# An RWKV-6 attention followed by a Hyena gate: the later two thirds of a hand-laid instruction order are laid anew, and the y of chunks 18 to 20 is transposed by DMA

## The chip, the core and the metric

The kernel runs on one core of a Trainium2 chip. The time is the device time of one execution in microseconds (us). Before the change it is 157.04 us, the median of three runs (156.68 to 157.12).

A core has TensorE (PE, matmuls and transposes; its weight loads are listed apart as PEld), VectorE (DVE), ScalarE (ACT), GpSimd (POOL), and SyncE (SP), which here only issues DMAs. Each engine works through its own instructions in program order; an instruction that depends on another engine's result waits for a semaphore, and everything behind it on its engine waits with it.

## What is computed

The inputs are r, k, v, w of shape (4, 8, 768, 48): 4 sequences (b), 8 heads, 768 time steps, head size 48. The first half is a recurrence with a decaying state:

```python
for t in range(S):
    cur = np.einsum('bhd,bhe->bhde', u[None] * kt, vt)
    y[:, :, t] = np.einsum('bhd,bhde->bhe', rt, state + cur)
    state = wt[:, :, :, None] * state + np.einsum('bhd,bhe->bhde', kt, vt)
```

Its output, laid out as x of shape (4, 768, 384), goes into the second half:

```python
proj = x @ w_proj
x1, x2, x3 = (proj[..., :D].copy(), proj[..., D:2 * D].copy(), proj[..., 2 * D:].copy())
X2 = np.fft.rfft(x2, n=S, axis=1)
H = np.fft.rfft(filter_fft, n=S, axis=0)[None, :, :]
x2_conv = np.fft.irfft(X2 * H, n=S, axis=1)
y = x1 * x2_conv * x3
return (y @ w_out).astype(np.float32)
```

## The kernel before, in words

**Tiling.** A sequence is cut into 6 chunks of 128 time steps, so there are 24 chunks, numbered 0 to 23; chunks 18 to 23 are the last sequence, b = 3. A chunk holds all 8 heads, 128 x 384 numbers.

**Chunk work.** For chunk c, four loads (`ldw`, `ldk`, `ldr`, `ldv`, 192 KB each, issued by SP) bring the inputs. ACT takes the logarithm of w (`lw`), PE sums it over time with triangular matrices (`cs`, `ce`), ACT exponentiates (`en`, `eq`, `ph`). `kh` and `q` multiply k and r by these factors, `rk` is r times k, `rku` multiplies by u, `cc` sums it per head, `v` casts v, `vc` is v times that sum. The pair q, kh is transposed: either eight PE transposes into PSUM (`tqk`) and a copy out (`tT` on ACT or DVE), or, for chunks 18 to 23 already before the change, one DMA transpose (`tT` issued by SP). Then `sc` (scores, PE, into a double-size PSUM tile that only `sc` and the last `pA` use), `mt` (masking, DVE, 1024 wide), `kv` and `S` (state on PE and DVE), `y` (PE), `xn` (DVE: y plus vc). `xn` is transposed by three PE transposes (`yt`) and copied into `xT` (ACT or DVE). In the second half of a sequence (chunks 3 to 5 of it) DVE also forms sum and difference with the first half, `sa` and `sb`, straight from the transpose's PSUM tile and from `xT` of the chunk three earlier.

**Sequence work.** For each sequence: `x2` (6 projections of the sums and differences) and `ab` (copies), a forward transform `f` (6 matmul groups), the products with the filter's spectrum `ur`, `ui` and their difference `pp`, the inverse transform `iE`, `iO`, `iP`, the copy `ec`, sum and difference `s`, `d`; beside it the projections `p1` and `p3` with `x1`, `x3` (copies) and `g` (their product); `yy` (or its halves `yl`, `yh`) multiplies by g; `po` (or `pA` with `pB`) is the output projection, `o` the copy out of PSUM and `st` the store. The suffix `.b.fb.hf` of p1 and p3 names sequence, column block and half of the time axis: `p3.3.2.0` is sequence 3, block 2, first half, and reads `xT` of chunks 18, 19 and 20.

**The order.** Nothing is a loop in the emitted program: the string `ORDER` (lines 42 to 141) lists 1103 words, and `emit` (lines 864 to 879) issues them one after the other. `V:mt23` is the operation `mt` on chunk 23 on DVE; P, V, A, G and S stand for PE, DVE, ACT, POOL and SP. `@3` names one of six PSUM banks (`@8` the double-size tile), `+2` adds warm-up matmuls. An operation that may run on several engines is moved by changing its letter. The order of words of one letter is the order on that engine. A PE operation into a bank waits until the readers of that bank's last tile are done; buffers in SBUF rotate (three of most chunk tiles, six load buffers of each input).

Names and lines that are touched: `op_xT` (692 to 699) has a branch for SP, one `dma_start_transpose` of the 128 x 384 tile `xn` into `xT`; `sums` (677 to 684) reads the transpose's PSUM tile for chunks 21 to 23 and `xT` for chunks 18 to 20; `op_tT` (592 to 599) is the DMA transpose of 128 x 1024 that exists before.

```python
        if e == "S":
            nc.sync.dma_start_transpose(
                out=xT_b[b % 2][:, :, ci * L:(ci + 1) * L], in_=xn_b[c % 3]
            )
            return
        copy(e, xT_b[b % 2][:, :, ci * L:(ci + 1) * L], bank_of[f"yt{c}"])
```

Of the kernel before, what the change touches and what calls it, by code (L numbers as in the profile page):

```python
# [53 lines left out]
G:vc2 A:xn1 V:S2 A:lw8 P:sc3@8+2 G:rk5 A:tT4 P:cs6@5 P:kv3@4 V:mt3 P:yt1@1 P:cs8@3 A:en6 G:kh5
P:y2@2 A:m2c5 V:xT1 P:ce6@5 V:cc4 G:vc3 P:sc4@8 A:v4 V:S3 A:xn2 G:vc4 V:mt4 A:en8 P:yt2@0+5
A:eq6 P:y3@1 G:rku5 A:xT2 S:ldv5 P:m2t1@4 V:q6 P:cs7@2 A:xn3 P:m2t4@3 G:kh6 P:ce8@0 A:en7 S:ldk7
P:ce7@1 V:m2c4 A:eq8 V:cc5 P:y4@2 A:eq7 V:rk6 P:m2t3@3 S:ldr7 A:ph7 A:m2c1 P:tqk5@1 A:xn4
P:tqk6@4 S:ldw9 A:tT5 P:yt3@2 V:fs S:ldv6 A:ph6 A:tT6 P:kv4@1 P:yt4@5 V:fd P:sc5@8 S:ldwp1
A:m2c3 G:kh7 V:sa4 P:hf4@4+5 V:sa3 V:S4 P:hf3@3 G:v5 V:sb3 A:ph8 V:sb4 A:lw9 P:hf1@1 S:ldr8
# [24 lines left out]
A:ab.1.0.1 V:cc12 P:yt11@0 S:ldr15 P:kv12@1 A:x1.1.2.0 P:x2.1.0.0@3 V:sa11 A:xT10 V:S12
P:iE.0.1@2 A:ab.1.0.0 S:ldv14 P:iO.0.1@4 V:sb11 G:q14 V:mt12 P:ce15@5 A:xT11 P:x2.1.0.2@1 A:lw17
S:ldv15 G:rku13 P:p1.1.2.1@3 A:eq15 V:rk14 P:ce17@0 P:sc13@8 A:x1.1.2.1 S:ldw18 P:iP.0.1 A:ph15
A:eq17 V:yy.0.0 G:rku14 P:x2.1.1.1@3 A:ab.1.0.2 V:cc13 S:ldr16 P:p1.1.0.1@5 A:v13 V:mt13
P:x2.1.1.2@0 A:ec.0.1 G:kh14 S:ldwo A:x1.1.0.1 P:kv13@1 A:ab.1.1.1 P:p1.1.1.1@2 V:s.0.1 G:q15
A:lw16 P:p3.1.2.0@5 V:S13 A:ab.1.1.2 P:f.1.0@3 V:d.0.1 A:x1.1.1.1 G:vc13 P:cs16@1 V:g.1.2.0
A:v14 P:cs17@0 P:ce16@4 V:ur.1.0 G:kh15 S:ldk16 A:en17 P:tqk14@2 A:en16 P:p3.1.0.0@5 A:tT14  # L90
V:yy.0.1 G:vc12 S:ldk17 P:y12@0 P:tqk15@1 V:cc14 P:p3.1.2.1@3 A:eq16 V:g.1.0.0 S:ldr17 G:rk15
A:v15 P:y13@2 V:tT15 A:ph16 P:kv14@5 A:lw18 V:xn12 P:sc14@8 S:ldk18 G:q16 P:cs18@4 V:xn13 A:cwo
P:f.1.2@1 V:g.1.2.1 S:ldw19 G:rku15 P:yt13@0 V:S14 P:yt12@2 A:en18 P:f.1.5@3 V:ur.1.1 A:xT13
G:rk16 S:ldv18 P:po.0.5@5 A:vc14 P:kv15@4 V:ui.1.2 P:po.0.4@0 G:kh16 S:ldv16 P:po.0.1@1 V:S15
G:rku16 P:p3.1.1.1@3 S:ldv17 V:mt14 A:o.0.4 P:po.0.3@4 A:o.0.5 G:kh18 P:f.1.4@0 S:ldw20 A:xT12
V:cc15 A:o.0.1 P:sc15@8 V:cc16 G:rk17 A:o.0.3 P:ce18@5 S:ldr18 P:y14@2 A:lw19 V:ur.1.2
P:po.0.0@1 A:eq18 G:rku17 S:ldk19 A:v18 P:tqk16@4 V:g.1.1.1 A:o.0.0 P:f.1.1@0 V:xn14 G:kh17
A:tT16 S:ldk20 P:ce19@3 V:mt15 P:yt14@1 P:f.1.3@2 A:xT14 G:vc15 S:ldr19 A:v16 P:cs19@4 V:ui.1.0
P:p3.2.1.0@1 G:q17 A:en19 P:sc16@8 S:ldw21 A:eq19 V:ui.1.1 P:p3.2.2.0@4 A:ph18 A:v17 G:vc16
P:y15@0 A:x3.2.1.0 S:ldv19 V:cc17 P:p1.2.1.0@5 A:lw20 G:q18 V:xn15 P:po.0.2@2 A:ph19 A:x3.2.2.0  # L100
S:ldr20 V:mt16 A:x1.2.1.0 P:tqk17@1 G:rk18 A:o.0.2 P:yt15@3 P:p1.2.0.0@0 S:tT18 A:tT17 V:sa15
P:ce20@4 V:pp.1.2 P:kv16@5 A:x1.2.0.0 V:pp.1.0 P:p3.2.0.0@2 G:kh19 A:eq20 V:sb15 S:ldw22
P:kv18@1 P:sc17@8 V:S16 A:lw21 P:y16@0 V:S18 A:ph20 G:vc17 A:xT15 S:ldw23 P:x2.2.1.0@5 V:mt17
A:x3.2.0.0 P:ce21@4 G:rku18 A:ab.2.1.0 P:iO.1.0@1 P:cs20@3 A:eq21 P:p1.2.2.0@2 V:xn16 A:en20
G:q19 P:p3.1.0.1@5 V:cc18 A:x1.2.2.0 P:y17@0 V:pp.1.1 A:ph21 A:vc18 G:rk19 S:tT19 P:yt16@3
P:iO.1.2@2 V:xn17 P:iE.1.2@4 V:sa16 P:iE.1.0@0 V:sb16 G:g.2.2.0 P:sc18@8 S:ldk21 V:g.1.0.1
P:iP.1.2 A:xT16 S:st.0.1 V:mt18 P:iP.1.0 G:q20 S:ldv20 A:ec.1.2 P:x2.2.0.0@5 S:ldv22 A:ec.1.0
P:yt17@3 P:x2.2.1.1@4 G:rku19 A:ab.2.0.0 V:s.1.2 A:v19 S:st.0.3 P:iE.1.1@0 V:s.1.0 P:iO.1.1@5
A:ab.2.1.1 G:rk20 V:sa17 S:ldr21 P:sc19@8 A:lw23 V:d.1.0 P:iP.1.1 A:lw22 V:sb17 P:kv19@4 G:kh20
V:d.1.2 S:ldv21 A:ec.1.1 P:x2.2.0.1@1 A:xT17 V:S19 P:cs21@2 G:yy.1.0 P:x2.2.1.2@0 A:ab.2.0.1  # L110
V:cc19 S:ldr22 A:en21 P:ce22@3 V:s.1.1 P:y18@4 A:ab.2.1.2 P:cs22@1 S:tT20 P:p1.2.0.1@2 V:xn18
A:v20 P:x2.2.0.2@0 A:eq22 V:d.1.1 G:vc19 A:x1.2.0.1 P:p3.2.2.1@4 V:mt19 A:ph22 A:ab.2.0.2
G:rku20 P:yt18@5 S:ldk22 P:cs23@2 A:en22 P:p1.2.2.1@3 A:x3.2.2.1 V:yy.1.1 G:rk21 P:kv20@0
# [818 lines left out]
```

## Time and profile before

| | |
|---|---|
| median of three runs | 157.04 us |
| the profiled execution | 157.1 us, of which 155.4 us from the first to the last instruction |
| busy: PE / DVE / ACT / POOL | 144.5 / 138.3 / 128.2 / 115.9 us |
| instructions: PE / DVE / ACT / POOL | 1540 / 264 / 306 / 134 |
| moved by DMA | 28.98 MB in 112038 packets, 106641 of them under 512 B |
| mean granted TensorE clock | 0.973 |

The busy time of an engine is the time in which at least one of its instructions runs. Instructions of one engine overlap a little (a matmul group that lasts 0.65 us is followed by the next 0.49 us after its start), so a busy share near 100% does not say that there is no short wait. SP is not counted as busy; its rows (SPq) show how long the issue of a DMA takes, and the listing of DMA issues shows how long it takes from the issue to the landing. The chain of waits follows the work that ended last back from its end: at each step to what released it, or to the instruction before it on its engine.

### The profile page before, as it was taken

The numbers are of one execution on the slowest core, as the hardware profiler recorded it, in microseconds if no ns is written. First come the engines' busy times: TensorE is split into PE (matmuls) and PEld (weight loads), VectorE is DVE, ScalarE is ACT, GpSimd is POOL, SyncE is SP. The second block draws the span as 40 slices with busy tenths as digits, with TensorE's granted clock in tenths as the row PEclk, the third lists the DMA queues.
The fourth block names the chain that finished last, engine by engine and source line by source line (L and its number), as shares of the span: only waits on it lengthen the run. The fifth ranks groups of instructions, "written<-read, shape, count | busy, mean of one in ns | idle before, by whom it ended". The sixth has DMA issues, their size and how long they took to land.

```text
span 155.4 us, 4177 instructions
## 1 busy us (share of the span) xinstructions
PE 144.5 (93%) x1540; PEld 90.8 (58%) x1540; DVE 138.3 (89%) x264; ACT 128.2 (82%) x306; POOL 115.9 (75%) x134
## 2 busy tenths in 40 slices
PE   6969988968999999999999999999999999999990
PEld 3446565756465666656757666775666566555440
DVE  6537879979989999999999999999999989999950
ACT  3279659969698899989999999999999877677470
POOL 7200869892999899799969999699999998900600
PEclk9985799999999999999999999999999999999997
DMA  5999979999999999899999999978999986000575
GB/s 96 196 202 183 207 148 197 195 286 226 244 172 281 253 178 200 170 192 211 190 200 259 170 181 210 189 147 141 227 209 228 206 175 222 2 0 0 181 281 203
DMA packets 112038, 28.98 MB, mean 186 GB/s; under 512 B 106641, under 2 KB 112018, under 8 KB 112018
## 3 DMA queue, kind: packets, MB, share of 16 engines
q1 hardware_dynamic: 112018, 28.72, 84.4%
q8 instruction: 12, 0.20, 0.6%
q14 instruction: 8, 0.07, 0.1%
HBM read 22.41 MB, written 4.72 MB: 175 GB/s over the span
## 4 chain that ended last, share of the span: by engine, by line
PE 63%; DMA 12%; DVE 11%; ACT 5%; SPq 5%; issue 2%; DVEq 0%
PE p L705 13%; DMA ldw<-in_w_dram 9%; PE x L735 6%; PE po L850 6%; PE f L421 5%; SPq L452 5%; PE sc L607 3%; PE f L413 3%; PE tqk L588 3%; DMA ldv<-in_v_dram 3%; PE iE L792 3%; PE iO L781 3%; PE iE L781 2%; PE yt L675 2%; DVE mt L614 2%
## 5 line engine op out<-in xcount | busy, mean ns | idle before, releaser
L505 POOL TENSOR_TENSOR qk<-ldr,eq 128x384 bf16<-128x384 f32 x20 | 21.3, 1067 | 11.4 <-ACT F L357 10.3
L705 PE MATMUL p<-xT,wproj 128*128 128x384 bf16 x144 | 29.3, 326 | 0.1
L614 DVE TENSOR_TENSOR mt<-sc,mask_excl 128x1024 bf16<-128x1024 f32 x24 | 29.2, 1216 | 0.0
L502 POOL TENSOR_TENSOR qk<-ldk,en 128x384 bf16<-128x384 f32 x21 | 22.4, 1067 | 4.1 <-PE kv L625 2.7
L508 POOL TENSOR_TENSOR rk<-ldr,ldk 128x384 bf16<-128x384 f32 x19 | 19.8, 1042 | 1.8 <-issue 1.5
L560 POOL TENSOR_TENSOR rku<-rk,u_bc 128x384 bf16<-128x384 bf16 x19 | 18.0, 945 | 2.5 <-DVE rk L508 1.3
L462 ACT ACTIVATE lg<-ldw 128x384 bf16<-128x384 f32 x24 | 12.6, 530 | 8.6 <-DMA ldw<-in_w_dram 7.5
L705 PEld LDWEIGHTS <-wproj 128*128 128x128 bf16 x144 | 13.0, 97 | 8.2 <-issue 1.0
L582 POOL TENSOR_TENSOR vc<-v,cc 128x384 bf16<-128x384 bf16 x19 | 16.5, 867 | 0.7 <-DVE cc L566 0.5
L757 DVE TENSOR_TENSOR filt<-f,HF 128x768 bf16<-128x768 f32 x18 | 16.6, 952 | 0.1
L735 PE MATMUL x<-wproj,sd 128*128 128x384 bf16 x72 | 14.9, 326 | 0.3 <-DVE HF L435 0.2
L276 ACT ACTIVATE qkT<-tqk 128x1024 bf16<-128x1024 bf16 x13 | 13.3, 1027 | 0.1
L276 ACT ACTIVATE v<-ldv 128x384 bf16<-128x384 f32 x23 | 12.2, 530 | 1.3 <-DMA ldv<-in_v_dram 1.3
L276 ACT ACTIVATE x<-p 128x384 bf16<-128x384 f32 x24 | 11.7, 499 | 1.8 <-PE p L705 1.6
L726 POOL TENSOR_TENSOR g<-g,x 128x384 bf16<-128x384 bf16 x8 | 7.1, 912 | 8.1 <-DVE g L278 8.1
L276 ACT ACTIVATE ab<-x 128x384 bf16<-128x384 f32 x24 | 11.7, 500 | 1.2 <-PE x L735 0.9
L484 ACT ACTIVATE en<-cs 128x384 f32<-128x384 f32 x24 | 11.9, 500 | 0.9 <-PE cs L466 0.7
L490 ACT ACTIVATE eq<-ce 128x384 f32<-128x384 f32 x24 | 11.5, 494 | 0.6 <-PE ce L478 0.6
L588 PE MATMUL tqk<-ident,qk 128*128 128x128 bf16 x144 | 11.5, 230 | 0.2 <-ACT phi L496 0.2
L632 DVE TENSOR_TENSOR S<-kv,phi 128x384 bf16<-128x384 f32 x20 | 10.9, 550 | 0.3 <-PE kv L625 0.2
L566 DVE TENSOR_REDUCE cc<-rku 128x8 f32<-128x384 bf16 x21 | 11.1, 541 | 0.0
L276 ACT ACTIVATE xT<-yt 128x384 bf16<-128x384 bf16 x20 | 9.9, 495 | 1.3 <-PE yt L675 0.6
(158 smaller groups left out, 397.0 us busy)
## 6 DMA issues: line engine op xcount, KB each, us to landing
ldw<-in_w_dram SPq DMA_DIRECT2D x24, 192.0 KB, 4.0
ldk<-in_k_dram SPq DMA_DIRECT2D x24, 192.0 KB, 4.2
ldr<-in_r_dram SPq DMA_DIRECT2D x24, 192.0 KB, 3.9
ldv<-in_v_dram SPq DMA_DIRECT2D x24, 192.0 KB, 4.0
out_dram<-o_all SPq DMA_DIRECT2D x24, 192.0 KB, 2.2
raw<-in_moe_w_proj_dram SPq DMA_DIRECT2D x3, 576.0 KB, 5.8
filt<-in_moe_filter_fft_dram SPq DMA_DIRECT2D x1, 1152.0 KB
P<-in_moe_w_out_dram SPq DMA_DIRECT2D x1, 576.0 KB, 5.0
```

What stands on the lines that cost most here:

```text
L276: nc.scalar.activation(out=o, in_=i, func=AF.Copy)
L462: nc.scalar.activation(out=o, in_=i, func=AF.Ln)
L502: two(e).tensor_mul(qk_b[c % 3][:, 1, :, 0:D], ld["k"][c % 6], en_b[c % 3])
L505: two(e).tensor_mul(qk_b[c % 3][:, 0, :, 0:D], ld["r"][c % 6], eq_b[c % 3])
L508: two(e).tensor_mul(rk_b[c % 2], ld["r"][c % 6], ld["k"][c % 6])
L560: two(e).tensor_mul(rku_b[c % 2], rk_b[c % 2], u_bc)
L582: two(e).tensor_mul(o, v, s.to_broadcast([L, H, D]))
L588: nc.tensor.transpose(p[:, x, j, :], qk_b[c % 3][:, x, 2 * j:2 * j + 2, :], ident)
L614: nc.vector.tensor_mul(mt_b[c % 3], bank_of[f"sc{c}"].rearrange("p q j t -> p (q j) t"), dataclasses.replace(m[:, :], ap=[m[:, :].ap[0], [ ...
L705: nc.tensor.matmul(p, wproj[:, cb, col0:col0 + L], xT_b[b % 2][:, cb, sl], start=(cb == 0), stop=(cb == CB - 1),)
L735: nc.tensor.matmul(p, sd_b[q][0][:, cb, ti * L:(ti + 1) * L], wproj[:, cb, C:2 * C], start=(cb == 0), stop=(cb == CB - 1),)
L757: two(e).tensor_mul(U_all[:, part, n], dataclasses.replace(f, ap=[f.ap[0], [0, 2]] + list(f.ap[1:])), HF[:, n, part:part + 2, :],)
```

## The change

Only the string `ORDER` changes. Its first 280 words, up to `A:ab.0.0.0`, stay in their order; in them 34 PE words, from `cs3` on, get other bank numbers. The 823 words behind them become 820 and are laid in another order on every engine. Three words are gone, `P:yt18`, `P:yt19` and `P:yt20`, nine PE transposes in all, and the words `A:xT18`, `A:xT19`, `A:xT20` become `S:xT18`, `S:xT19`, `S:xT20`. Other words that change engines, from the first letter to the second:

- ACT to POOL: v7, v13, vc14, vc18. ACT to DVE: ab.3.0.0, x1.3.0.1, x3.3.2.1, o.3.2, o.3.3.
- DVE to ACT: xT6, tT15, xT22, X.3.4, x3.3.1.1, ec.3.0, o.3.0.
- DVE to POOL: rku8, pp.0.1, q11, rk14, pp.1.0, g.2.1.0, g.3.0.1, g.3.1.0, g.3.2.1, yl.3.1, yh.3.1.
- POOL to DVE: pp.0.0, q13, rk13, yy.0.2, rku17, rk18, rku18, q20, g.2.0.1, g.3.1.1, yl.3.0.

The banks, the beginning of the new part, and the stretches in which the DMA transposes stand, before and after:

```diff
-G:rk3 V:cc0 V:rT1 P:sc1@8 V:vc0 S:ldw7 P:kv0@0 G:q4 P:rt2@4 P:cs3@3 P:m2t2@1 V:rT2 P:cs4@2 A:en3
+G:rk3 V:cc0 V:rT1 P:sc1@8 V:vc0 S:ldw7 P:kv0@0 G:q4 P:rt2@4 P:cs3@1 P:m2t2@2 V:rT2 P:cs4@3 A:en3
...
-P:x2.0.1.0@3 A:ab.0.0.0 V:cc7 P:sc7@8 A:v7 V:sb5 P:x2.0.0.1@0 S:ldr9 V:xn6 G:rk8 P:x2.0.0.2@2
+P:x2.0.1.0@4 A:ab.0.0.0 S:ldr9 G:rk8 S:ldv8 S:ldw10 P:x2.0.0.2@0 A:ab.0.1.0 P:x2.0.0.1@3 G:q8
...
-P:p3.2.1.1@4 V:xn19 P:po.1.1@5 V:ui.2.2 G:rku21 S:tT21 P:p3.2.0.1@0 P:sc20@8 V:ur.2.2 G:rk22
-A:x3.2.0.1 P:po.1.3@1 S:st.0.0 A:o.1.1 P:yt19@3 V:mt20 S:ldr23 P:po.1.4@0 G:pp.2.2 A:xT19
-S:st.0.5 P:kv21@2 A:o.1.3 S:ldk23 P:f.2.0@5 V:cc21 A:o.1.4 P:y20@3 V:ur.2.0 A:vc21 P:po.1.2@1
-G:kh22 P:po.1.0@0 V:xn20 P:po.1.5@5 G:q22 V:S21 P:yt20@3 P:sc21@8 V:pp.2.0 A:xT20 G:rku22
-P:f.2.2@2 S:tT22 A:o.1.2 V:mt21 A:o.1.0 P:f.2.3@3 A:x3.2.1.1 P:p1.3.1.0@1 G:q23 S:ldv23 V:ur.2.1
-P:p1.3.2.0@0 A:x1.3.1.0 G:kh23 P:y21@4 A:o.1.5 P:iO.2.0@1 A:v22 V:xn21 P:p1.3.0.0@2 G:rk23
-S:tT23 V:ui.2.1 P:iO.2.1@5 A:x1.3.0.0 P:yt21@4 P:sc22@8 A:x1.3.2.0 V:sa21 G:rku23 P:iE.2.1@2
...
+A:ab.2.1.1 V:xn18 P:p1.2.0.1@3 V:s.1.0 S:xT18 P:p1.2.2.1@4 G:rku20 A:x1.2.0.1 V:d.1.0 P:iO.1.1@0
+A:v20 V:d.1.2 P:kv19@3 G:yy.1.0 A:lw23 S:tT20 P:iE.1.1@5 V:cc20 A:x1.2.2.1 P:p3.2.2.1@2 V:cc19
+A:x1.2.1.1 P:sc19@8 V:S19 S:ldk22 P:iP.1.1 V:yy.1.2 P:x2.2.1.2@4 G:rk21 S:ldr22 A:ec.1.1 V:mt19
+P:p3.2.0.1@1 A:x3.2.2.1 S:st.0.0 P:kv20@3 A:x3.2.0.1 S:ldk23 P:x2.2.0.1@5 G:vc19 V:s.1.1
+A:ab.2.1.2 P:ce22@2 S:st.0.5 A:ab.2.0.1 V:S20 P:ce23@1 G:rku21 P:f.2.4@4 S:st.0.4 A:eq22 V:d.1.1
+P:sc20@8 S:st.0.1 A:ph22 V:ur.2.2 G:kh21 A:eq23 P:f.2.1@5 S:ldv21 A:vc20 P:y19@3 V:yy.1.1 G:kh22
+P:f.2.5@0 V:xn19 P:po.1.0@2 V:mt20 S:xT19 P:cs23@1 P:p3.2.1.1@4 G:q22 A:en23 P:po.1.5@3 A:o.1.0
+V:cc21 P:po.1.4@1 A:x3.2.1.1 G:kh23 S:tT21 V:ui.2.2 A:o.1.5 P:y20@2 A:o.1.4 P:po.1.2@4 G:rk22
+V:xn20 P:f.2.0@3 A:v21 V:ui.2.0 S:xT20 P:f.2.3@0 G:rk23 A:vc21 V:ur.2.0 P:f.2.2@1 G:pp.2.2
+P:kv21@2 S:st.0.3 P:po.1.1@5 V:ui.2.1 S:tT22 P:po.1.3@3 A:o.1.1 V:S21 P:sc21@8 V:ur.2.1 G:q23
+P:p3.3.2.0@0 S:ldv22 P:p3.3.1.0@5 S:st.0.2 V:mt21 G:rku23 P:p1.3.2.0@2 S:tT23 A:x3.3.1.0
+P:p1.3.0.0@1 A:x1.3.2.0 G:rku22 P:p1.3.1.0@5 V:cc23 A:x1.3.0.0 S:ldv23 V:pp.2.0 P:y21@2
+G:g.2.0.0 A:x1.3.1.0 P:sc22@8 S:st.1.5 V:xn21 A:o.1.3 P:p3.3.0.0@1 A:x3.3.2.0 S:st.1.0 V:mt22
...
+P:iP.2.1 G:g.3.1.0 P:y22@4 A:ec.2.0 P:x2.3.1.0@5 A:ec.2.1 V:xn22 G:vc23 P:y23@1 A:ab.3.1.0
+V:s.2.1 P:iE.2.2@0 G:g.2.2.0 P:yt22@4 V:xn23 P:iO.2.2@5 P:iP.2.2 V:sa22 G:g.2.1.1 V:d.2.1
```

More of the change, by code (lines that the diff above doesn't have):

```diff
@@ L54 @@
[L54 to L59, printed above, removed]
@@ L84 @@
[L84 to L89, printed above, removed]
@@ L90 @@
[L90 to L113, printed above, removed]
@@ new lines @@
+A:ab.0.0.2 V:xn6 P:ce9@1 A:ab.0.0.1 P:sc7@8 V:sb5 S:ldwp2 V:cc7 P:yt6@4 A:xT5 G:rku8 P:f.0.1@0
+V:mt7 A:eq9 P:x2.0.1.1@2 A:xT6 G:v7 P:tqk8@3 A:cwp0 G:kh9 V:ui.0.0 P:x2.0.1.2@5 S:ldw13
+P:f.0.0@4 A:ab.0.1.2 G:rk9 V:cc8 P:kv7@0 A:ab.0.1.1 V:ur.0.0 P:p1.0.0.1@5 S:ldr10 A:ph9 A:v8
+G:vc7 P:f.0.2@2 A:lw10 V:pp.0.0 S:ldk10 A:x1.0.0.1 P:f.0.3@1 G:rku9 A:tT8 V:ur.0.1 P:f.0.5@4
+S:ldw11 P:p1.0.0.0@5 G:q9 V:ui.0.1 P:y7@3 A:x1.0.0.0 P:p1.0.1.0@2 S:ldw12 A:cwp2 V:xn7 G:vc8
+P:p1.0.2.1@5 V:ui.0.2 P:yt7@1 S:ldk11 P:f.0.4@3 G:pp.0.1 A:x1.0.1.0 P:sc8@8 A:xT7 V:S7 P:ce10@4
@@ new lines @@
+P:y14@1 P:f.1.4@0 V:ur.1.0 S:ldk18 G:vc14 A:cwo P:tqk16@3 V:ur.1.2 P:p3.1.1.1@4 G:rku16 S:ldw22
+P:ce18@2 A:tT16 P:sc15@8 V:xn14 G:rk17 P:po.0.2@0 V:S14 S:ldr18 A:v15 P:yt14@1 V:g.1.1.1
+P:po.0.4@3 A:eq18 G:q17 V:mt15 A:xT14 P:po.0.1@5 S:ldw20 A:o.0.4 P:kv15@4 A:lw19 G:kh17
+P:p1.2.0.0@1 V:cc15 S:ldk19 A:v16 P:sc16@8 V:pp.1.2 A:ph18 A:o.0.2 G:vc15 P:tqk17@3 A:x1.2.0.0
+V:mt16 S:ldk20 P:p3.2.2.0@2 A:o.0.1 P:y15@0 G:kh18 A:x3.2.2.0 P:ce19@1 S:ldv17 V:S15 A:tT17
+P:p1.2.1.0@5 V:rku17 G:pp.1.0 P:cs19@2 P:f.1.3@4 V:xn15 S:ldr19 A:eq19 V:cc16 A:en19 P:f.1.2@3
@@ new lines @@
+V:ui.1.1 A:x1.2.1.0 S:ldv18 P:p3.2.1.0@0 A:ph19 A:lw21 P:kv16@2 G:q18 V:ur.1.1 A:x3.2.1.0
+P:p3.2.0.0@5 S:ldr20 A:lw22 P:yt15@1 P:po.0.3@4 A:lw20 V:S16 G:vc16 S:tT18 P:y16@0 V:sa15
+A:o.0.3 V:rk18 P:cs22@3 G:kh19 P:sc17@8 A:v17 V:sb15 P:ce20@2 V:xn16 A:xT15 P:p3.1.0.1@4 V:rku18
+A:eq20 G:q19 S:ldv20 P:po.0.5@0 A:x3.2.0.0 V:cc17 P:po.0.0@1 A:o.0.5 S:ldv19 V:g.1.0.1
+P:p3.1.2.0@5 A:ph20 A:v18 G:vc17 V:mt17 P:cs21@0 A:o.0.0 P:p1.2.2.0@2 S:ldw23 A:en22 G:rk19
+P:x2.2.1.0@4 A:x1.2.2.0 V:g.1.2.0 P:cs20@1 P:y17@3 S:ldr21 V:q20 A:en20 G:rku19 P:ce21@2 V:xn17
@@ L141 @@
+V:s.3.1 P:iP.3.2 S:st.2.5 V:d.3.0 G:yl.3.1 P:po.2.1@3 V:d.3.1 A:ec.3.2 P:po.2.4@4 V:yl.3.0
+A:o.2.1 G:yh.3.0 V:s.3.2 P:po.2.3@1 A:o.2.4 S:st.2.1 P:pA.3.2@0 V:yl.3.2 A:o.2.3 G:yh.3.1
+P:pA.3.0@5 S:st.2.4 V:d.3.2 P:pB.3.0 P:pB.3.2 S:st.2.3 P:pA.3.1@3 A:o.3.0 V:o.3.2 P:pB.3.1
+P:pA.3.4@8 S:st.3.0 V:yh.3.2 A:o.3.1 P:pB.3.4 S:st.3.2 P:pA.3.3@4 A:o.3.4 S:st.3.1 P:pB.3.3
+A:o.3.5 V:o.3.3 S:st.3.4 S:st.3.3 S:st.3.5
 """
```

99 lines of the change are left out of this document (52 added, 47 removed).

## The prediction

> **What bounds the kernel now.** I read the page's shares first, then the stretches of the later two thirds, then the chain of waits backwards from its end.
>
> The page: busy times, the DMA slices, shares of the chain, and two rows of the DMA issues (last figure: median us from issue to landing).
>
> ```profile
> PE 144.5 (93%) x1540; PEld 90.8 (58%) x1540; DVE 138.3 (89%) x264; ACT 128.2 (82%) x306; POOL 115.9 (75%) x134
> DMA  5999979999999999899999999978999986000575
> PE 63%; DMA 12%; DVE 11%; ACT 5%; SPq 5%; issue 2%; DVEq 0%
> ldv<-in_v_dram SPq DMA_DIRECT2D x24, 192.0 KB, 4.0
> out_dram<-o_all SPq DMA_DIRECT2D x24, 192.0 KB, 2.2
> ```
>
> The stretch from the first re-laid word to the end of the last score masking (mt of chunk 23), and from there to the last copy (us, busy time of each engine, clock, DMA share, GB/s):
>
> ```profile
> 47.10:131.04 83.94, 83.47 (x953) 53.98 (x953) 82.30 (x139) 79.51 (x201) 78.24 (x79) 1.00 0.96 204
> 131.04:151.76 20.72, 20.13 (x151) 10.79 (x147) 18.45 (x44) 13.92 (x31) 7.98 (x10) 1.00 0.25 89
> ```
>
> In 83.9 us PE is busy 83.5, DVE 82.3, ACT 79.5, POOL 78.2, and the DMA engines 96%. Nothing stands idle, so a new order has little idle time to win, and what is moved off one engine lands on another that is almost as full. The granted clock is 1.00 throughout, so it is no term of the sum.
>
> The chain from 115.9 us to the end (start, duration, what):
>
> ```profile
> 115.90 0.49 PE f L421 x3
> ...
> 118.78 0.17 PE yt L675 x3
> ...
> 131.26 0.33 PE iO L781 x2
> ...
> 132.99 0.49 PE x L735 x3
> ...
> 151.00 0.18 PE pA L842
> 151.18 0.02 issue
> 151.20 0.56 DVE o_all L278
> ```
>
> It never leaves PE from 115.90 to 151.18: over the last 35 us PE runs from one group to the next, and no other engine ends a wait that lasts. Here too are the paces of PE (start to start): 0.49 for a projection of three matmuls, 0.33 for an inverse half, 0.17 for the three transposes of one y.
>
> **The change, part by part.** I counted the words of each engine in both orders and gave each the duration of its own row. DVE, POOL and ACT groups, from 47.9 us on (busy us, mean ns of one | idle before):
>
> ```profile
> L771 DVE TENSOR_TENSOR P<-filt 128x768 bf16<-128x768 bf16 x9 | 5.9, 675 | 0.0
> L812 DVE TENSOR_TENSOR raw<-raw,g 128x768 bf16<-128x768 bf16 x7 | 3.9, 566 | 0.2
> L505 DVE TENSOR_TENSOR qk<-ldr,eq 128x384 bf16<-128x384 f32 x1 | 0.9, 887 | 0.0
> L278 DVE COPY xT<-yt 128x384 bf16<-128x384 bf16 x2 | 0.7, 342 | 0.0
> L278 DVE COPY qkT<-tqk 128x1024 bf16<-128x1024 bf16 x1 | 0.7, 681 | 0.0
> L508 DVE TENSOR_TENSOR rk<-ldr,ldk 128x384 bf16<-128x384 f32 x1 | 0.6, 550 | 0.0
> L560 DVE TENSOR_TENSOR rku<-rk,u_bc 128x384 bf16<-128x384 bf16 x1 | 0.5, 533 | 0.0
> L757 DVE TENSOR_TENSOR filt<-f,HF 128x768 bf16<-128x768 f32 x18 | 16.6, 952 | 0.1
> ```
> ```profile
> L560 POOL TENSOR_TENSOR rku<-rk,u_bc 128x384 bf16<-128x384 bf16 x15 | 14.3, 954 | 2.5 <-DVE rk L508 1.3 <-DVE cc L566 1.0
> L582 POOL TENSOR_TENSOR vc<-v,cc 128x384 bf16<-128x384 bf16 x13 | 11.2, 859 | 0.6 <-DVE cc L566 0.5
> L771 POOL TENSOR_TENSOR P<-filt 128x768 bf16<-128x768 bf16 x3 | 4.9, 1640 | 0.6 <-DVE filt L757 0.6
> ```
> ```profile
> L276 ACT ACTIVATE v<-ldv 128x384 bf16<-128x384 f32 x16 | 8.5, 530 | 0.0
> L276 ACT ACTIVATE xT<-yt 128x384 bf16<-128x384 bf16 x17 | 8.4, 496 | 1.3 <-PE yt L675 0.6 <-DVE sd L690 0.4
> L578 ACT ACTIVATE vc<-v,cc 128x48 bf16<-128x48 bf16 x32 | 7.6, 326 | 0.1
> ```
>
> *Bank numbers in the first third.* The order there stays and each bank's former tile is emptied no later than before, so I take 0. A bank that came free late would cost at most one ACT copy, 0.5 us; as PE also waits for other things, 0 to 0.5.
>
> *PE.* Three transposes of y fall away: 3 x 0.17 = 0.5 us less. Nothing is added.
>
> *ACT.* Less: xT 18 to 20 (3 x 0.496), v7 and v13 (2 x 0.530), vc14 and vc18 (32 short instructions for four chunks took 7.6, so 1.9 each), five copies of some 0.5 in the tail. More: tT15 (1.0) and six copies. Net 4.8 us less. ACT does not stand in the late chain, so I count 0 of it; if its copies free PSUM banks earlier, that is the second rival.
>
> *POOL.* rku8, vc14, vc18, pp.1.0 and two v come to it, yy.0.2, rku17, rku18, rk18 and q20 leave; with the tail some 2.5 us more in all, about 1 of it ahead of the last vc. It is idle 83.94 - 78.24 = 5.7 us in the stretch, which covers that; without the cover vc comes late for xn, at 1 us.
>
> *DVE.* Ahead of mt23 five words are added: yy.0.2 0.566, rku17 and rku18 2 x 0.533, rk18 0.550, q20 0.887, together 3.07. Four leave: tT15 0.681, rku8 0.533, one pp 0.675, xT6 0.342, together 2.23. q, rk and pp words that only trade places cancel. Net +0.8 ahead of mt23. In the tail four short products, a store copy and others leave, and five copies and products come: some 0.9 less behind mt23. DVE's total does not change, but its work is moved ahead of the hand-over to PE.
>
> *The hand-over at the end.* DVE and PE around it, by start and duration (the L668 row is xn20, the first L614 row mt21, the second mt23; the PE rows begin y21 and y23):
>
> ```profile
> 121.17 0.55 DVE L668 TENSOR_TENSOR xn<-y,vc 128x384 bf16<-128x384 f32 x1
> ...
> 122.63 1.23 DVE L614 TENSOR_TENSOR mt<-sc,mask_excl 128x1024 bf16<-128x1024 f32 x1
> ...
> 129.83 1.21 DVE L614 TENSOR_TENSOR mt<-sc,mask_excl 128x1024 bf16<-128x1024 f32 x1
> ```
> ```profile
> 122.19 0.40 PE L607 MATMUL sc<-qkT 48*128 48x128 bf16 x8
> ...
> 124.60 0.21 PE L640 MATMUL y<-S,qkT 128*128 128x96 bf16 x1
> ...
> 131.43 0.20 PE L640 MATMUL y<-S,qkT 128*128 128x96 bf16 x1
> ```
>
> mt23 ends at 131.04 now and y23 starts 0.4 later, when PE is free: PE decides. With 0.8 more ahead, and DVE's own waits as they are, mt23 ends at 131.9. PE has less ahead of y23: 0.5 for the transposes, and one projection and one inverse half moved behind y23 against one projection moved ahead, 0.3; it is ready at 131.43 - 0.8 = 130.6 and waits. So y23 starts 0.45 later, with 0.3 more work behind it: the end moves by +0.8.
>
> *The DMA transposes.* The transpose that exists, from the rows of its line (issue, ns min/median/max; then us to landing, min/median/max):
>
> ```profile
> L594 SPq DMA_TRANSPOSE qkT<-qk x6: 1238/1547/1996, 98.5 to 125.4; - x6
> DMA to landing us min/median/max: 3.0/3.8/4.1
> ```
>
> xT is three eighths of its size. No row shows this size; its landing lies between a store's 2.2 and 4.1 us. I take 3.0, nearest to the tT rows, which use the same path. xT18 and xT19 have the same first reader, p3.3.2.0, and are issued 3 us or more earlier, which hides them. xT20 is the tight one: xn20 ends at 121.72 now; with +0.8 and the two L757 products that move behind it (2 x 0.95, less their overlap) it ends at about 120.9. xT20 lands at 123.9 (123.1 to 125.0). p3.3.2.0, the first reader, follows sc21 directly; PE reaches it near 123.0, and its bank (0) is free only after ui.2.1, three L757 products after xn20, at 123.5. So PE stalls 0.4 for the landing (0 to 1.5). Five projections then lead to y21 at 126.3, 1.7 later than now, with three projections fewer behind it (1.5): +0.2, and +1.3 if it lands at 125.0. This runs beside the hand-over and is not added to it; the later of the two sets the end.
>
> [...]
>
> *The SP queue.* Now xn18 on DVE, two issues of loads (the first is ldv21) and the start of kv21:
>
> ```profile
> 111.17 0.56 DVE L668 TENSOR_TENSOR xn<-y,vc 128x384 bf16<-128x384 f32 x1
> ```
> ```profile
> 110.42 0.70 SPq L452 DMA_DIRECT2D ldv<-in_v_dram  x1
> ...
> 114.09 0.58 SPq L452 DMA_DIRECT2D ldk<-in_k_dram  x1
> ```
> ```profile
> 119.27 0.33 PE L623 MATMUL kv<-S,ident 128*128 128x384 bf16 x1
> ```
>
> xT18 waits for xn18. Six DVE words of about 0.47 (cc19, S19, two s, two d) move behind xn18 and 0.9 comes ahead of it, so it ends near 111.73 - 1.9 = 109.8. Behind xT18 stand tT20, ldk22, ldr22, four stores, ldk23 and ldv21. With 0.5 to 0.6 for an issue and 1.5 for tT20, ldv21 issues at about 115.8 and lands 4.0 later at 119.8; v21 (0.53) is ready at 120.3. kv21 has 2 us more PE work ahead of it than now (three f, three po and y20 come ahead, two po and two yt go) and starts near 121.3. The cover is 1 us, so I take 0.
>
> Sum: the profiled execution's 157.1 us + 0.8 (hand-over) = 157.9; its 157.1 lies 0.06 over the median, so 157.8 for the median.
>
> **The rivals.**
>
> *The DMA queue takes the place.* With an issue of 2.0 for each of xT18 and tT20 and a landing of 4.1, ldv21 arrives 1.7 later than above, kv21 stalls 0.7, and xT20 then holds tT22, ldv22 and tT23 behind it: together with xT20's +1.3 the end moves by about +2.0: 159.1. For it: DMA slices at 8 and 9 up to 131 us, and one SP queue. Against it: the last loads have 3 us to spare on the way to y23.
>
> *Faster: PE decides, not DVE.* The deciding point is mt23 before 130.6. From 47.1 on 105 groups at 0.49, 24 halves at 0.33 and the shorter words at their paces in the chain add up to some 98 us, and PE takes 151.18 - 47.1 = 104, so some 6 us are short waits. If ACT's 4.8 us spare empties banks earlier and takes 0.7 us off these, DVE too is fed earlier, and mt23 no longer holds PE. Then -0.5 (transposes) - 0.7: 155.9. For it: the chain is all PE. Against it: DVE's 98% in the stretch.
>
> *No change.* The new waits and the saved transposes cancel (-0.5 against +0.5): 157.1.
>
> **How the numbers follow.** Slower by the hand-over 0.40 (157.3 to 158.5 on its own), by the DMA queue 0.14, no change 0.19, faster 0.27. A change of 0.3% (0.5 us) is about what a measurement of this kernel can tell from none. Some of the hand-over case lies within that, and some of the no-change case outside it: faster 0.29, same 0.20, slower 0.51. The range for 8 in 10 goes from 155.8 (the faster rival) to 159.3 (the queue rival and a little of the bank bound).
>
> **What would show it.** Right: mt23 ends later than 131.3, y23 follows it at once, and the chain steps from PE to DVE between 120 and 134 us. The transpose step is right if p3.3.2.0 starts within 0.5 us of ui.2.1's end and xT lands in about 3 us. Wrong if mt23 ends before 130.6, if PE's late chain has loads or xT in it for over 1 us, or if POOL's vc ends the waits of xn.

## The result and the profile after

The changed kernel takes 158.25 us (median of 20 runs, 156.87 to 161.31) and the kernel before 156.91 us (20 runs, 155.90 to 158.03) on the same chip: a ratio of 1.0084, 95% interval 1.0059 to 1.0110. The change makes the kernel 0.8% slower. On two other chips the same comparison gave 1.0142 (1.0087 to 1.0197) and 1.0125 (1.0073 to 1.0177). Medians are of all executions, while a ratio leaves out those more than 1.5% above the fastest of their kernel on that chip, so it need not be the quotient of the two medians beside it.

The first profile of the changed kernel is of the longest of these executions (161.31 us); the lines below are from a later one, e1b, of 157.65 us. From the page: busy times, the DMA slices, the shares of the chain.

```profile
PE 142.5 (91%) x1531; PEld 89.4 (57%) x1531; DVE 140.8 (90%) x262; ACT 123.3 (79%) x287; POOL 120.1 (77%) x138
DMA  5999999999999999999899898992799794003493
PE 35%; DVE 28%; POOL 12%; issue 8%; DMA 7%; ACT 5%; SPq 2%; POOLq 0%; DVEq 0%; ACTq 0%
```

ACT moved as the counts said (4.9 us less); POOL has 4.2 us more, where 2.5 were counted. PE's 2.0 us less lie in the first third: in the two stretches below it is busy for 103.8 us, before for 103.6. VectorE is 2.5 us busier (1.2 against a second profile of before), which the counts did not say, and the chain has 28% of VectorE where it had 11%. The DMA row ends in 3493 where it ended in 0575: the last slices are fuller.

The same two stretches as before the change, from 0.5 us into x2.0.1.0, the last PE group of the unchanged first third, to the end of mt23, and from there to the last copy (us, busy time of PE, PEld, DVE, ACT, POOL, clock, DMA share, GB/s):

```profile
44.43:130.11 85.68, 83.55 (x946) 53.16 (x945) 85.29 (x141) 75.04 (x182) 80.90 (x83) 1.00 0.95 200
130.11:151.21 21.10, 20.22 (x145) 10.81 (x143) 17.96 (x40) 14.07 (x32) 9.89 (x11) 1.00 0.27 97
```

Up to mt23 VectorE now stands idle for 0.4 us of 85.7; it was 1.6 of 83.9. PE waits for 2.1 us there instead of 0.5. PE's waits of over 0.15 us in this stretch (who waits, for whom: total, times, longest), before and changed:

```profile
PE cs L466 <- DVE g L728: 0.2, 1, 0.2
```
```profile
PE yt L675 <- DVE xn L668: 1.0, 3, 0.5
PE po L850 <- DVE xn L668: 0.5, 1, 0.5
PE po L850 <- DVE raw L812: 0.4, 1, 0.4
PE tqk L588 <- ACT xT L276: 0.2, 1, 0.2
```

So PE waits for VectorE's xn and yy (L812) for 1.9 us, where it waited 0.2. The chain, late part:

```profile
113.77 0.96 DVE filt L757
114.73 1.33 DVE raw L812
116.11 0.50 PE po L850 x2
...
122.42 2.53 PE p L705 x15
124.95 0.98 DVE P L771
125.92 0.48 DVE xn L668
126.45 0.34 PE yt L675 x3
...
147.91 0.35 PE pA L842
148.48 2.05 DMA out_dram<-o_all
150.65 0.56 DVE o_all L278
```

Two things are to be seen. Between 113 and 126 us the chain steps from PE to VectorE and back. And the end is no longer PE's: a copy into o_all (150.65) waits for a store that was issued at 148.48 and had to land first. mt23 (L614) and the start of y23 (the first L640 row):

```profile
128.90 1.21 DVE L614 TENSOR_TENSOR mt<-sc,mask_excl 128x1024 bf16<-128x1024 f32 x1
```
```profile
130.21 0.21 PE L640 MATMUL y<-S,qkT 128*128 128x96 bf16 x1
```

y23 starts 0.1 us after mt23's end at 130.11; it was 0.4 before. The absolute times can't be set beside those of before: the first third, whose words are the same in all kernels here, puts the group x2.0.1.0 anywhere between 43.8 and 48.3 us in the profiles. What can be compared is the length of pieces. In the table, "middle" is the first stretch above, "y23 to PE" goes from the start of y23 to the end of PE's last group, "PE to land" from there to the landing of the last store (issue plus landing of the single stores). "Packet" says whether an instruction packet (8 KB; the trace lists it among the DMA packets as "q14 instruction") was read while the last three stores ran, "last lands" is the landing time of the last store.

| kernel | middle | DVE busy in it | y23 to PE | PE to land | packet | last lands |
|---|---|---|---|---|---|---|
| before (page) | 83.94 | 82.30 | 19.74 | 3.11 | no | 2.07 |
| before, again | 84.92 | 83.79 | 19.74 | 3.37 | no | 2.08 |
| changed, first profile | 84.94 | 84.50 | 20.15 | 4.21 | yes | 2.89 |
| changed, e1 | 85.91 | 84.58 | 20.13 | 4.41 | yes | 2.88 |
| changed, e1b (shown above) | 85.68 | 85.29 | 20.15 | 4.19 | yes | 2.89 |
| e2 own slots | 85.82 | 84.54 | 20.15 | 3.97 | yes | 2.86 |
| e3 three DVE words less | 84.96 | 83.31 | 20.13 | 3.11 | no | 2.01 |
| e4 before, y by DMA | 87.75 | 84.43 | 19.74 | 3.44 | no | 2.07 |
| e5 order only | 84.81 | 84.27 | 19.85 | 4.17 | yes | 3.07 |
| e6 tail of before | 83.29 | 82.73 | 20.41 | 3.08 | no | 2.06 |
| e6b, again | 84.29 | 83.42 | 20.41 | 3.08 | no | 2.07 |
| e8 before, tail of changed | 84.61 | 82.91 | 19.95 | 3.09 | no | 1.98 |
| e9 two stores less | 85.07 | 84.11 | 20.52 | 4.04 | yes | 2.92 |
| e10 words back on POOL | 84.92 | 84.24 | 19.95 | 4.00 | no | 2.06 |

### The profile page after: what moved, and what is told of

It is laid out like the page before. It is cut to its first block, busy times and chain, and to the rows that moved or that the text cites. A ratio compares the mean times of both kernels' runs of the same rounds, so it can differ in the third digit from the quotient of the medians.

```text
span 159.6 us, 4165 instructions
## 1 busy us (share of the span) xinstructions
PE 144.7 (91%) x1531; PEld 90.9 (57%) x1531; DVE 140.3 (88%) x262; ACT 123.9 (78%) x287; POOL 119.7 (75%) x138
## 4 chain that ended last, share of the span: by engine, by line
PE 39%; DVE 26%; DMA 13%; SPq 6%; issue 5%; POOL 4%; ACT 3%; DVEq 0%; ACTq 0%; POOLq 0%
PE p L705 7%; DMA ldv<-in_v_dram 6%; DVE mt L614 6%; SPq L452 6%; PE x L735 6%; DMA ldw<-in_w_dram 5%; DVE filt L757 5%; PE po L850 5%; PE f L421 3%; DVE xn L668 3%; PE f L413 2%; PE iE L792 2%; PE iE L781 2%; PE iO L781 2%; DVE raw L812 2%
## 5 line engine op out<-in xcount | busy, mean ns | idle before, releaser
L614 DVE TENSOR_TENSOR mt<-sc,mask_excl 128x1024 bf16<-128x1024 f32 x24 | 29.1, 1210 | 0.0
L582 POOL TENSOR_TENSOR vc<-v,cc 128x384 bf16<-128x384 bf16 x21 | 18.0, 858 | 3.8 <-DVE cc L566 2.0
L508 POOL TENSOR_TENSOR rk<-ldr,ldk 128x384 bf16<-128x384 f32 x18 | 18.6, 1036 | 1.8 <-DMA ldr<-in_r_dram 1.8
L560 POOL TENSOR_TENSOR rku<-rk,u_bc 128x384 bf16<-128x384 bf16 x18 | 17.4, 970 | 2.2 <-DVE rk L508 1.7
L726 POOL TENSOR_TENSOR g<-g,x 128x384 bf16<-128x384 bf16 x10 | 9.0, 921 | 7.9 <-DVE g L278 7.9
L276 ACT ACTIVATE qkT<-tqk 128x1024 bf16<-128x1024 bf16 x14 | 14.3, 1022 | 0.6 <-PE tqk L588 0.5
L276 ACT ACTIVATE v<-ldv 128x384 bf16<-128x384 f32 x21 | 11.1, 529 | 2.6 <-DMA ldv<-in_v_dram 2.6
L276 ACT ACTIVATE xT<-yt 128x384 bf16<-128x384 bf16 x19 | 9.3, 494 | 3.4 <-DVE sd L690 2.6
L276 ACT ACTIVATE x<-p 128x384 bf16<-128x384 f32 x23 | 11.0, 496 | 1.0 <-PE p L705 0.9
L850 PE MATMUL po<-wout,raw 128*128 128x384 bf16 x54 | 10.9, 326 | 0.9 <-DVE xn L668 0.5
L276 ACT ACTIVATE ab<-x 128x384 bf16<-128x384 f32 x23 | 10.8, 497 | 0.7 <-PE x L735 0.3
```

Source lines behind the costliest of these rows:

```text
L276: nc.scalar.activation(out=o, in_=i, func=AF.Copy)
L508: two(e).tensor_mul(rk_b[c % 2], ld["r"][c % 6], ld["k"][c % 6])
L560: two(e).tensor_mul(rku_b[c % 2], rk_b[c % 2], u_bc)
L582: two(e).tensor_mul(o, v, s.to_broadcast([L, H, D]))
L614: nc.vector.tensor_mul(mt_b[c % 3], bank_of[f"sc{c}"].rearrange("p q j t -> p (q j) t"), dataclasses.replace(m[:, :], ap=[m[:, :].ap[0], [ ...
L850: nc.tensor.matmul(p, y_b[b % 2][:, cb, ti * L:(ti + 1) * L], wout[:, cb, :], start=(cb == 0), stop=(cb == CB - 1),)
```

## The experiments

The theories: the *hand-over* (VectorE has more ahead of mt23), the *tail* (the late stores of sequence 2 hold the end), and the *DMA queue* (transposes of y hold loads or PE).

**e1, the changed kernel again.** No edit.

> The changed kernel itself, for its time and a second profile. Before to after was 156.9 to 158.2 us. Hand-over theory (DVE has more work ahead of mt23, and PE waits for it): mt23 ends 0.8 to 1.0 us later than in before (131.04), y23 starts within 0.2 us of its end, and the last TensorE group ends about 0.8 to 1.1 later than 151.17. Tail theory (the stores of sequence 2 are issued so late that the last copies wait for their landings in the same slots of o_all): from the end of the last TensorE group to the last landing it is 4.2 us against 3.1 in before, so some 1.1 us of the loss lies behind TensorE's last group.

159.64 us, 1.0142 of before. mt23 ends at 131.39 and y23 starts 0.1 after it; PE's last group ends at 151.62. PE to land is 4.41. The tail is there in every profile of the changed kernel; the middle floats by 1 us.

**e2, own slots for the last copies.**

```diff
+    def o_slot(b, ti):
+        if b == 3:
+            return ld["k"][ti].rearrange("p h d -> p (h d)")
+        return o_all[:, ti, :]
...
-        copy(e, o_all[:, ti, :], bank_of[f"po.{b}.{ti}"])
+        copy(e, o_slot(b, ti), bank_of[f"po.{b}.{ti}"])
...
-        nc.sync.dma_start(out=out[b, ti * L:(ti + 1) * L, :], in_=o_all[:, ti, :])
+        nc.sync.dma_start(out=out[b, ti * L:(ti + 1) * L, :], in_=o_slot(b, ti))
```

> The changed kernel, same order, but sequence 3's output tiles go through the slots of the dead k loads, so that no copy o.3.x waits for a store of sequence 2. Tail theory: the waits of the last copies on store landings go (1.4 and 1.6 us in the profile of after) and the time falls by 0.5 to 1.1 us, to about 157.3. Hand-over theory alone: mt23 and the last TensorE group are where they were, the last stores only queue behind the others, and the time moves by less than 0.3 us.

159.37 us, 1.0119 (1.0076 to 1.0162): within 0.3 us of e1. The waits of the copies on landings are gone (the last copy ends 0.6 after PE's last group instead of 1.1), but PE to land falls only from 4.41 to 3.97. The waits alone are not the tail: the last five stores, which no longer wait, land in 2.9 to 3.0 us each.

**e3, less work on VectorE ahead of mt23.** The words V:rku17, V:rk18 and V:rku18 are taken out of the order.

> The changed kernel without three words that the change laid onto VectorE ahead of mt23: rku17, rku18 (0.533 each) and rk18 (0.550). These products are left out, so chunks 17 and 18 take stale values; everything else is as in after. Hand-over theory: 1.6 us less of DVE work ahead of mt23, so mt23 ends at least 0.8 us earlier and the time falls by 0.8 to 1.2 us (157.0 to 157.4), until TensorE decides. Tail theory: the end behind TensorE's last group keeps its 4.2 us, so the time falls no more than the last group does. DMA queue theory: ldv21 and xT20 decide, and the time moves by less than 0.3 us.

159.02 us, 1.0106 (1.0046 to 1.0166), 0.6 us below e1 with wide intervals. Its profile speaks against the hand-over as I had put it: the middle is 84.96 us, no shorter than in the first profile of the changed kernel. Of the time that VectorE saved it waited 1.0 us again:

```profile
DVE xn L668 <- PE y L646: 0.5, 2, 0.3
DVE g L728 <- PE p L705: 0.3, 1, 0.3
DVE filt L757 <- PE f L413: 0.2, 1, 0.2
```

(from its waits between 90 and 130 us: total, times, longest; the changed kernel shows none there). But the tail, which the edit doesn't touch, fell from 4.41 to 3.11. That was in no theory, and it is what led on to the instruction packet.

**e4, the kernel before with y of chunks 18 to 20 by DMA.**

```diff
-... P:y18@4 ... V:xn18 ... P:yt18@5 ... A:xT18 ...
+... P:y18@4 ... V:xn18 S:xT18 ...
```

> The kernel before, with its own order, and only the transposes of y of chunks 18 to 20 by DMA (issued on SP right behind xn18, xn19, xn20; the three groups of TensorE and three ScalarE copies gone). Hand-over theory: the transposes neither stall nor help: within 0.4 us of before. DMA queue theory: SP waits for xn18 with loads behind it, ldv21 lands late and kv21 or sc21 stall: 0.6 us or more slower than before. If TensorE's work alone set the end: 0.5 us faster (3 x 0.17).

161.00 us, 1.0205 (1.0145 to 1.0265): 3.4 us slower than before, more than any theory gave. The chain shows it (xn20 at 121.71, then):

```profile
121.71 0.54 DVE xn L668
122.25 0.47 DVE S L632
122.72 0.66 DVE P L771
123.37 3.41 DMA xT<-xn
126.83 1.15 PE p L705 x6
```

xn20 ends at 122.25, SP issues xT20 only at 123.37, behind tT21, two stores and two loads, and it lands 3.41 later. PE, which in this order has a projection of sequence 3 next, waits 1.8 us for it. Another 1.0 us of PE's waits, a little earlier, is for a PSUM bank whose copy (ACT, o_all) had itself waited for a store to land (PE's waits from 110 to 135 us):

```profile
PE p L705 <- DMA xT<-xn: 1.8, 1, 1.8
PE po L850 <- ACT o_all L276: 1.0, 1, 1.0
```

So the transposes by DMA are not free; in the changed kernel the new order is what hides them. In e1b (rows of the transposes' line: issue, first and last start; then landing):

```profile
L695 SPq DMA_TRANSPOSE xT<-xn x3: 1178/1186/1187, 108.0 to 119.5; - x3
...
DMA to landing us min/median/max: 2.3/2.4/3.7
```

xT20 is issued at 119.46, right behind xn20, and lands at 121.77, before ui.2.1 ends (122.03). PE runs the scores sc21 from 122.02 and p3.3.2.0 from 122.35, right behind them: it does not wait for the transpose.

**e0, the kernel before again**, for a second profile.

> The kernel before once more, for a second profile beside those of the others. All theories: as the first profile, with PE's last group ending near 151 and 3 to 3.2 us from there to the last landing.

155.71 us in one run. Its marks from 63 to 112 us (mt9 to mt19) stand 2.1 us earlier than in the first profile; 0.8 of that is lost between xn18 and xn19 (see the last section), and PE's groups from y21 to the last stand 1.64 earlier.

**e5, the new order without the transposes by DMA.**

```diff
-... S:xT18 ... S:xT19 ... S:xT20 ...
+... P:yt18@3 ... A:xT18 ... P:yt19@3 ... A:xT19 ... P:yt20@2 ... A:xT20 ...
```

> The changed kernel with its new order, but y of chunks 18 to 20 transposed on TensorE and copied by ScalarE again (three groups of 0.17 us and three copies of 0.5 us back, three issues of 1.2 us gone from SP). If the transposes by DMA cost the time (they cost 3 us in the order of before), this is 0.8 us or more faster than the changed kernel, near 157.5 or less. If the new order alone costs it (hand-over and tail), it stays within 0.6 us of the changed kernel; the three groups make it 0.5 slower where TensorE decides.

157.21 us against 156.85 of before on that chip, 0.2% by the medians; the ratio is 1.0132 (1.0087 to 1.0177), as large as the changed kernel's, but it goes back to five of before's 23 executions (153.82 to 155.94). The changed kernel itself was not run on that chip, so the time does not settle how much of the loss goes with the order and how much with the transposes. The profile says more: PE to land is 4.17, as in the changed kernel, so the longer end does not need the transposes. The 0.5 us that PE saves by them can't be seen in the time.

**e6, the changed kernel with the tail of before.** The words behind sb23 (118 of them, from 132 to 134 us on) stand in before's order on before's engines.

```diff
-... S:st.2.5 ... A:o.2.1 ... A:o.2.4 S:st.2.1 P:pA.3.2@0 ... S:st.2.4 ... S:st.2.3 P:pA.3.1 ...
+... S:st.2.3 ... S:st.2.1 ... A:o.2.5 ... P:pA.3.1 ... A:o.2.4 S:st.2.5 P:pA.3.2 ... S:st.2.4 ...
```

> The changed kernel up to the last sd word of chunk 23 (about 134 us), and from there the order, engines and stores of before, transposes by DMA kept. Tail theory (nine stores of 0.54 us each follow one another from 149 us and end 4.4 us behind the last TensorE group in the changed kernel): the end behind TensorE's last group shrinks to 3.1 to 3.4 us and the time falls by 0.8 to 1.4 us. Hand-over theory alone: mt23 and y23 are where they were, and the time moves by less than 0.3 us.

1.0021 (0.9976 to 1.0066), again with those five of before's executions; by the medians it is 157.68 us against 156.85. Once more on another chip, beside the changed kernel:

> The changed kernel with the tail of before once more, beside the changed kernel on one chip. Tail theory: 0.8 to 1.4 us faster than the changed kernel and within 0.4% of before. Theory that the middle costs the time: as slow as the changed kernel.

156.98 us, 1.0052 (0.9999 to 1.0106), where the changed kernel had 158.35 us:

> The changed kernel once more, beside the two swaps on one chip: 0.8 to 1.4% slower than before; y23 to the last landing 24.4 us by the tail theory, whatever the time of y23 is.

1.0125 (1.0073 to 1.0177). So on this chip 1.4 us of the loss goes with the tail's order. On the first chip the ratio points the same way (1.0021 against e5's 1.0132), the medians do not (157.68 against e5's 157.21 us), and the changed kernel itself was not run there. PE to land is 3.08 in both profiles, and neither has a packet among the last stores, so the swap took away more than an order of stores.

**e8, the kernel before with the tail of the changed kernel.**

> The other half of the swap: the kernel before up to the last sd word of chunk 23 (no transposes of y by DMA), and from there the order, engines and stores of the changed kernel. Tail theory: 4.1 to 4.4 us from the end of TensorE's last group to the last landing (3.1 to 3.4 in before), y23 to the last landing 24.0 to 24.5 us instead of 22.9 to 23.1, and 0.8 to 1.4 us slower than before. Theory that the re-laid middle (hand-over, transposes) costs the time: within 0.4 us of before.

157.31 us against 156.56: 1.0063 (1.0027 to 1.0098), 0.75 us slower, just under what the tail theory expected. But its profile does not show the tail: PE to land is 3.09. The word order alone does not make it. Where the 0.75 us of this kernel lie, its one profile does not show, and that stays open.

**e9, two stores less.** S:st.2.4 and S:st.2.3 are taken out.

> The changed kernel without two of the nine stores that close it (tiles 3 and 4 of sequence 2 are left out of the output). If the transfers of the stores themselves hold the end (0.54 us of all DMA engines each), the last landing comes 0.9 to 1.1 us earlier after TensorE's last group: 3.1 to 3.4 us instead of 4.2 to 4.4. If the copies or a fixed latency hold it, it stays above 4.

PE to land is 4.04, not 3.1 to 3.4: the transfers of nine stores are not what holds the end (and e3, with all nine, has 3.11). The time was 157.32 us, 1.0051 (1.0018 to 1.0084), below e1b's 1.0125. The end does not account for that: from y23 to the last landing this profile has 24.6 us and e1b's 24.3. Its middle is 0.6 shorter, which is within what single profiles differ by; why the time is lower stays open. The rows of its last 7 us of DMA (busy tenths and GB/s in 40 slices of 149 to 156 us) hold the answer:

```profile
DMA  0089999999979889980029971000000000000000
GB/s 0 9 307 386 334 395 360 369 378 351 369 272 407 316 290 369 342 290 18 18 105 369 395 264 44 26 9 0 0 0 0 0 0 0 0 0 0 0 0 0
...
q14 instruction: 1, 0.01, 0.7%
```

Near 152.3 and again near 153.4 the transfers go on at 9 to 44 GB/s, a sixteenth or so of the 369 around them. The trace notes sixteen updates of a semaphore for the landing of each store, and a store has landed with the last of them (the last store of before: from 1.91 to 2.07 us after the issue, landed at 2.07). Of the last store here fifteen come within 0.2 us, up to 2.51 after the issue, and the sixteenth at 2.92: one of sixteen parts is behind the others. An instruction packet (8 KB, the q14 row) was read at 151.2, in the middle of these stores. The changed kernel (e1b) in 149 to 155 us has the same end, with some 0.8 us at 20 to 31 GB/s, and one packet, at 152.4:

```profile
GB/s 389 358 389 338 338 420 379 338 379 379 369 338 379 369 369 348 379 369 359 348 348 400 403 348 318 369 379 358 113 31 21 20 31 20 0 0 0 0 0 0
...
q14 instruction: 1, 0.01, 0.3%
```

In the table above, all six profiles with a packet among the last stores have the last landing at 2.9 to 3.1 us, and all eight without at 2.0 to 2.1. In the six the sixteenth update of the last store comes 0.4 to 0.8 us behind the fifteenth, in the eight at most 0.04.

**e10, the words back on POOL.** A forecast from that: e3 differs from the changed kernel by three VectorE instructions only, and its packet came behind the end, so I took the packet's time to go with VectorE's instructions, an estimate from this one pair; with three fewer in another way it should come behind the end too. (Counted with their waits, VectorE's instructions in the trace are 323 in each of the six profiles with the packet among the last stores, and 311 to 320 in the eight without.)

```diff
-... V:yy.0.2 ... V:rku17 G:pp.1.0 ... V:rk18 ... V:rku18 ...
+... G:yy.0.2 ... G:rku17 V:pp.1.0 ... G:rk18 ... G:rku18 ...
```

> The changed kernel with yy.0.2, rku17, rk18 and rku18 back on POOL and pp.1.0 back on VectorE, as before has them: three instructions fewer on VectorE, order and tail as they are. Theory of the instruction fetch (in the changed kernel an 8 KB instruction packet is read while the last stores run, one of the 16 DMA engines then falls back by 1 us, and in the run without three VectorE words it came after the end): the last packet before the end lies behind the last landing, the last three stores land in 1.9 to 2.1 us instead of 2.9 to 3.2, TensorE's last group to the last landing is 3.0 to 3.4 us, and the time falls by 0.7 to 1.1 us. Theory of the nine stores' transfers: 4.0 to 4.4 us as it is. Hand-over theory: 2.8 us less of work on VectorE ahead of mt23 and 2.9 us more on POOL; y23 comes up to 0.5 earlier if VectorE set it, later by up to 1 us if POOL's vc17 or vc18 come late.

The packet came at 156.2, behind the last landing at 155.0. The last three stores (start, landing) and the rows of the DMA in 149 to 156 us:

```profile
L859 SPq DMA_DIRECT2D out_dram<-o_all x3: 332/333/406, 151.9 to 153.0; - x3
...
DMA to landing us min/median/max: 2.1/2.1/2.1
```
```profile
GB/s 0 0 0 0 281 334 395 351 369 395 334 386 377 334 369 386 360 377 351 386 351 369 369 342 386 369 360 377 342 395 369 281 18 0 0 0 0 0 0 0
```

against 2.9 to 3.2 in e1b:

```profile
L859 SPq DMA_DIRECT2D out_dram<-o_all x3: 332/332/405, 150.6 to 151.7; - x3
...
DMA to landing us min/median/max: 2.9/3.0/3.2
```

The trickle at the end is gone, and all sixteen updates of the last store come within 0.2 us, by 2.06. This part held. But PE to land is 4.00, not 3.0 to 3.4: now the last copy waits longest for the landing of st.2.3 and ends 1.5 us after PE's last group. In time, 1.0039 (0.9995 to 1.0083; the medians are 158.95 and 157.80 us). So the tail of the changed kernel has two causes that lie beside each other. Take away the waits of the copies (e2) and 3.97 are left by the packet; take away the packet (e10) and 4.00 are left by the waits; with no packet and short waits (e3), or with the tail of before (e6), it is 3.1. Own slots and no packet at once, in the changed kernel's order, wasn't tried. No version here beats the kernel before: e6, the nearest, is within what its intervals can tell from it.

## Why the prediction was right, and where it was not

The number held: 157.8 forecast, 158.25 measured, slower as given the most chance. The sum behind it held in part; one term was too uncertain to be confirmed and a whole term was missing, so that the number came so near is in part luck: the loss forecast was 0.8 us and the one measured is 1.3 to 2.0.

- *Behind y23, 0.3 us more PE work*: right. y23 to PE's last group is 20.13 to 20.15 in three profiles of the changed kernel and 19.74 in both of before: 0.40. It is not the count of words alone: e5 and e10, with the same PE words behind y23, take 19.85 and 19.95.
- *The hand-over moves to VectorE*: the mechanism was right. y23 follows mt23 in 0.1 us instead of 0.4, the chain steps to VectorE between 113 and 126 us, and in seven profiles with the changed kernel's words up to mt23 (e1, e1b, e2, e6, e6b, e9, the first one) the middle goes with VectorE's busy time: 83.29 with 82.73, 84.29 with 83.42, up to 85.68 with 85.29 and 85.91 with 84.58. PE's waits for VectorE in the middle are 0.5 to 1.9 us in these seven and 0.2 to 0.6 in three with before's words. The sign as it was written, mt23 later than 131.3, can't be used: mt23 ends at 133.76, 131.39 and 130.11 in three profiles of the changed kernel, because the first third takes longer in some executions.
- *Its size, +0.45*: not settled. The mean middle is 85.0 us in those seven profiles and 84.5 in three with before's words (the two of before and e8), but single ones lie up to 2.6 us apart. e3, without three of the moved words, has no shorter middle than the mean. "With DVE's own waits as they are" was the weak half-sentence: they are not, they come back.
- *The price of the words moved to VectorE*: mis-sized. rk18 was counted at 0.550 and took 1.31 to 1.32 in the eight profiles that have it on VectorE in this place; yy.0.2 was counted at 0.566 and took 0.9 to 1.3 in five of them. POOL works beside the long ones: in e1b rk18 runs from 97.07 for 1.31 and a kh word on POOL from 96.97 for 1.00 (see also the last section). q20 was mis-sized the other way: counted at 0.887, it took 0.54 in all eight. The five added words, 3.07 by the count, took 3.7 to 4.3. VectorE's work ahead of mt23 was forecast 0.8 longer; its busy time there is 1.2 longer by the same means (84.2 against 83.0).
- *The transposes by DMA*: right in the outcome, not in the step. Landing was put at 3.0 and was 2.3 to 3.7, 2.3 for xT20, the one that counts. The stall of 0.4 did not come: xT20 lands 0.3 before ui.2.1 ends in e1b and 0.2 before in e1, and that p3.3.2.0 starts 0.3 behind ui.2.1 is the scores sc21 running ahead of it. The end of the range did not come either, and e4 shows that the same three transposes cost 3.4 us where the order does not hide them: the rival with the DMA queue was a real danger, which the order avoids.
- *The SP queue*: right in its outcome. In e1 ldv21 was issued at 116.35 (forecast 115.8) and landed 4.46 later, v21 started at once, kv21 at 121.87 (forecast 121.3), 0.5 us behind it. The cover was 0.5 instead of 1.
- *PE, 0.5 us less by the transposes*: not visible; e5, which puts them back, does not settle it.
- *The tail*: the step that was missing. The working let the end follow PE's last group "+0.8" and counted only VectorE's and PE's words there. It did not follow the stores: three of sequence 2 are issued behind 147.5 us, right ahead of the six of sequence 3, which use the same slots. From PE's last group to the last landing is 1.0 us longer (4.2 to 4.4 against 3.1 to 3.4): 0.8 in the landing of the last store, the rest in copies that wait for landings. The waits of ACT and of VectorE in 147 to 152 us, before and changed (total, times, longest):

```profile
DVE o_all L278 <- PE pA L842: 1.6, 1, 1.6
...
ACT o_all L276 <- DMA out_dram<-o_all: 0.3, 1, 0.3
```
```profile
DVE o_all L278 <- ACT o_all L276: 1.4, 1, 1.4
ACT o_all L276 <- DMA out_dram<-o_all: 1.5, 2, 0.8
```

Before, the last copies wait for PE; now for landings. (VectorE's 1.4 us are put down to ACT, but the chain above has the landing of the store issued at 148.48 as what its copy waited for.) By the profiles what lies behind y23 (0.4 of PE and 1.0 after it) is enough for the 1.3 us measured first; the 2.0 and 1.8 us on the other two chips leave room for 0.4 to 0.6 in the middle, and its means differ by 0.5. The swap of the tail gives back most of it where the changed kernel ran beside it (e6b). So the number came out near with one term confirmed (0.3), one not settled (0.45) and one of 1.0 that it did not have.

The bank renaming was not tried alone. Among the rivals, "no change" and "faster" are excluded by the interval, and the DMA queue's place by the rows of ldv21 and p3.3.2.0.

## What to carry to other kernels

When an order is laid anew, the sum has to go on to the last landing: list the stores that are still to be issued when the bound engine ends, which slots their successors need, and what else the DMA engines read at that time. Price a word that moves to VectorE not by its mean row alone (rk18: 0.55) but by what POOL does at that moment (1.31 beside a kh word). And compare pieces of profiles (from one mark to the next), since the start of a kernel may float by more than the change is worth.
